# Six of sixteen score tiles a head take another way from PSUM to the exponential: bfloat16 scores, a GpSimd add, one exponential for two tiles

## The chip, the cores and the metric

The program runs on one core of one Trainium2 chip. The metric is device time in microseconds (us), the median of several runs. A profile is one execution taken by the hardware profiler; its times count from the start of that execution's span.

## The reference

A transformer block on 2048 rows of 640 numbers: a layer norm with a conditioned scale and shift, attention with 32 heads of width 128 against a cache of 2048 keys and values, a gated residual, and then a second part with a mixer and an MLP, which the change doesn't touch. What matters here is the attention:

```python
q = (x @ wq).reshape(B, Sq, H, Dh).transpose(0, 2, 1, 3)
scores = jnp.einsum('bhqd,bhkd->bhqk', q, k_cache) * Dh ** (-0.5)
p = _softmax(scores, axis=-1)
o = jnp.einsum('bhqk,bhkd->bhqd', p, v_cache)
return o.transpose(0, 2, 1, 3).reshape(B, Sq, H * Dh) @ wo
```

Inputs and weights are bfloat16. The softmax is taken as exp(score - maximum); its sum comes out of the product with the values, to which a column of ones is appended, and the division follows at the end.

## The kernel before, in words

The kernel is written for the five engines' own queues. A helper class `Prog` keeps a list of operations for each engine in the order in which the program text adds them, and derives every wait from the keys that an operation reads (`r=`) and writes (`w=`). An engine runs its list strictly in order, so an operation that waits holds back all that stands behind it on that engine.

**Loop.** The attention is one loop over steps `s` (L552). There are 32 heads with 16 tiles each, 512 tiles in all; a tile is 128 queries against all 2048 keys. Step `s` starts tile `s` and finishes tile `s - PVD` with `PVD = 8`. I call tiles by their place in the head, 0 to 15. In step `s` each engine gets:

- **TensorE**: for each of two halves of the keys, the scores of tile `s` (two 128x512 matmuls, L301 and L15, into a half of the PSUM tile `Sps`), the product of the probabilities of tile `s - 8` with half of the values (eight matmuls, L314), and a piece of other work where one is due: a fifth of the next head's query projection (L246) or four 128x128 transposes (L262). The scores' half may only be overwritten when VectorE has read it.
- **VectorE**: for each half, one instruction (L594) that reads 1024 columns of scores from PSUM, multiplies by -SCALE, writes them as float32 into `negS`, and accumulates the minimum of them. `negS` has three slots, used in turn, one a tile. So the write of tile `s` waits until the exponential of tile `s - 3` has read its slot.
- **GpSimd**: the smaller of the two halves' minima (L604), 128x1. Further down in the step, the normalisation of a finished tile: L462 for each tile, before the first of four L455 (a reciprocal), after the last of four L469, a store to DRAM.
- **ScalarE**: at every second step the copy of two finished output tiles out of PSUM (L585, into `Of`), then evacuations of queries (L253) and transposed probabilities (L271) where they are due, then the exponential of tile `s` (L607): it reads `negS` with scale -1 and the minimum as bias (a 128x1 operand), and writes bfloat16 probabilities into slot `s % 10` of the ring `Pb`.
- **SyncE** issues the DMA transposes of the probabilities (L231) from `Pb` to the ring `PTs`, for two tiles at once where the two are neighbours, else for one.

**Tiles transposed by TensorE.** In each head tiles 3 and 10 are transposed by TensorE; in every fourth head (`h % 4 == 1`) tile 2 as well. `PE_STEPS` says at which step. Each such tile has two evacuations of 1024 columns: most by ScalarE (L271); VectorE does the second one of tile 2 and of tile 3 (L273, by `by_dve`), 40 in all.

The order of the work is thus written out by hand: nothing is reordered by a scheduler. After the loop come the output projection and the second part of the block.

Of the kernel before, what the change touches and what calls it, by code (L numbers as in the profile page):

```python
# [7 lines left out]
ACT = mybir.ActivationFunctionType  # L8
# [115 lines left out]
def bass_adaLN_cond__mha_block_cached__mixer_s_mlp__prompt_kernel(  # L124
# [7 lines left out]
    NQT = SQ // 128  # L132
# [13 lines left out]
    with ExitStack() as es:  # L146
# [11 lines left out]
        if True:  # L158
            with ExitStack() as es1:
                sb1 = lambda name, shape, dt: es1.enter_context(nc.sbuf_tensor(name, shape, dt))  # L160
                RP = 10
                PVD = 8
                PE_STEPS = ({3: 6, 10: 13}, {2: 5, 3: 7, 10: 14})
                kind = lambda h: 1 if h % 4 == 1 else 0
                US = KT * (SQ + 4)
                sb1("pad", [128, 32], F32)
                ring = sb1("ring", [128, 2 * RP, SK], BF16)
                negS = sb1("negS", [128, 3, SK], F32)
                wo = sb1("wo", [128, H, D], BF16)
                kv = sb1("kv", [128, 2 * SK + 2 * NKT * 130 + 2 * KT * 128 + 2 * SQ], BF16)  # L170
                small = sb1("small", [128, 4 * NQT + 32], F32)
                hTx = sb1("hTx", [128, US], BF16)
                Of = sb1("Of", [128, 4, 2, 130], F32)
# [4 lines left out]
                nm0, nm1, nm, rl = [small[:, 4 * NQT + 8 * i:4 * NQT + 8 * i + 8] for i in range(4)]  # L178
# [8 lines left out]
                Pb = ring[:, 0:RP]  # L187
# [22 lines left out]
                G = Prog(nc, es1, "a")  # L210
# [61 lines left out]
                    else:  # L272
                        G.op("vector", lambda v: v.tensor_copy(dst, src), r=[("J", jb)], w=[("PT", g % RP, r)])  # L273

                by_dve = lambda g, r: r == 1 and g % NQT in (2, 3)
                PIECES = []
                for steps in PE_STEPS:
                    taken = [u for j in steps.values() for u in range(2 * j, 2 * j + 4)]
# [68 lines left out]
                if H > 1:  # L347
# [8 lines left out]
                     r=["id0"], w=["ident"])  # L356
# [3 lines left out]
                for k in range(KT):  # L360
                    G.op("gpsimd", lambda g, k=k: g.tensor_scalar(out=s_bc[:, k, :], in0=ones_f, scalar1=c_f[:, k:k + 1],
                                                                  scalar2=1.0, op0=ALU.mult, op1=ALU.mult),
                         r=["onesf", "cf"] + WRK, w=[("sbc", k)])
# [78 lines left out]
                def mod_rows(i):  # L442
                    n0, n1 = MROW[i]
                    bank = PO[:, (i % 2) * 512:(i % 2) * 512 + n1 - n0]

                    def f(t):
                        for k in range(KT):
                            ins = t.matmul(bank, s_bc[:, k, :], wmodr[:, k, n0:n1], start=(k == 0), stop=(k == KT - 1))
                        return ins
                    G.op("tensor", f, r=[("sbc", k) for k in range(KT)] + [("wm", 1)] + WRK, w=[("O", i % 2)])  # L450
                    G.op("scalar", lambda a: a.copy(mod_bc[:, n0:n1], bank), r=[("O", i % 2)], w=[("mod", i)])
# [35 lines left out]
                w2 = negb[:, 2 * H * 128:2 * H * 128 + KT * D].rearrange("p (k n) -> p k n", k=KT)  # L487
                us = hTx[:, 0:US].rearrange("p (k q) -> p k q", k=KT)
                nT = kv[:, 0:KT * SQ].rearrange("p (t k q) -> p t k q", t=NQT, k=KT)
# [59 lines left out]

                YB = [Sps[:, 0:1024], Sps[:, 1024:2048]]  # L550
                LAG = 4
                for s in range(NG + PVD + LAG):  # L552
                    h, j = divmod(s, NQT)
                    g_ = s - PVD
                    evacs = []
                    if s <= 2:
                        for i in ((0,), (1, 2), range(3, len(MROW)))[s]:
                            mod_rows(i)
                    if s == 3:
                        G.op("gpsimd", lambda g: g.tensor_scalar(  # L560
                            out=mod_bc[:, 2 * D:3 * D], in0=mod_bc[:, 2 * D:3 * D], scalar1=1.0, scalar2=1.0, op0=ALU.add, op1=ALU.mult),
                            r=[("mod", i) for i in range(len(MROW))], w=["mod"])
                    for half in range(2):
                        if s < NG:
                            qk(s, half)
                        if half == 0 and s in (NG + PVD - 5, NG + PVD - 4):
                            b0 = a_pe(0, None if s == NG + PVD - 5 else b0, (s - NG - PVD + 5,))
                        if half == 0 and s == NG + PVD - 2:
                            b1 = a_pe(1, None, (0,))
                        if 0 <= g_ < NG:  # L570
                            pv(g_, half)
                        if s == 0 and half == 1:
                            q_head0(NQC - 1)
                        if h + 1 < H and 2 * j + half in PIECES[kind(h)]:
                            cc, q = PIECES[kind(h)][2 * j + half]
                            q_piece(h + 1, cc, q)
                            if q == KT - 1:
                                evacs.append((q_evac, h + 1, cc))
                        for g, r in t_of(s):
                            t_piece(g, r, half)  # L580
                            if half == 1:
                                evacs.append((t_evac, g, r))
                    if 0 <= g_ < NG and g_ % 2 == 1:
                        p = g_ // 2
                        G.op("scalar", lambda a, p=p: a.copy(  # L585
                            Of[:, p % 4].rearrange("p z d -> p (z d)")[:, 0:259], PO[:, (p % 2) * 512:(p % 2) * 512 + 259]),
                            r=[("O", p % 2)], w=[("Of", p % 4)])
                    for fn, x, y in evacs:
                        if fn is q_evac or not by_dve(x, y):
                            fn(x, y)  # L590
                    for half in range(2):
                        if s < NG:
                            r8 = s % 8
                            G.op("vector", lambda v, half=half, s=s, r8=r8: v.tensor_scalar(  # L594
                                out=negS[:, s % 3, half * 1024:(half + 1) * 1024],
                                in0=Sps[:, half * 1024:(half + 1) * 1024],
                                scalar1=-SCALE, scalar2=None, op0=ALU.mult, op1=ALU.min,
                                accum_out=(nm0 if half == 0 else nm1)[:, r8:r8 + 1]),
                                r=[("S", half)], w=[("negS", s % 3), ("nmh", half, r8)])
                    for fn, x, y in evacs:  # L600
                        if fn is t_evac and by_dve(x, y):
                            fn(x, y)
                    if s < NG:
                        G.op("gpsimd", lambda g, r8=r8: g.tensor_scalar(  # L604
                            out=nm[:, r8:r8 + 1], in0=nm0[:, r8:r8 + 1], scalar1=nm1[:, r8:r8 + 1], scalar2=None, op0=ALU.min),
                            r=[("nmh", 0, r8), ("nmh", 1, r8)], w=[("nm", r8)])
                        G.op("scalar", lambda a, s=s, r8=r8: a.activation(  # L607
                            Pb[:, s % RP, :], negS[:, s % 3, :], ACT.Exp, bias=nm[:, r8:r8 + 1], scale=-1.0),
                            r=[("negS", s % 3), ("nm", r8)], w=[("Pb", s % RP)])
                        if not is_pe(s):  # L610
                            if s % 2 == 1 and not is_pe(s - 1):
                                transpose(s - 1, 2)
                            elif s % 2 == 1 or is_pe(s + 1):
                                transpose(s, 1)
                        if j == 2 and h >= 1 and h + 1 < H:
                            load_k(h + 1)
                        if h + 1 == H and j in (2, PVD + 1):
                            i = 0 if j == 2 else 1
                            load_ot(0, OTC[i], OTC[i + 1], i)
                        if j == 6 and h + 2 < H:  # L620
                            load_wq(h + 2)
                        if j == PVD + 1 and h + 1 < H:
                            load_v(h + 1)
                    if 0 <= s - PVD - LAG:
                        gr, z = divmod(s - PVD - LAG, 4)
                        if z == 0:
                            rcp(gr)
                        norm(gr, z)
                    if s == NG:
                        G.op("gpsimd", lambda g: g.memset(mhalf, -0.5), w=["mhalf"] + NEG)  # L630
                        load_ot(0, OTC[2], OTC[3], 2)
                        load_xt(0, 1)
                        load_ot(1, 0, H // 2, 0)
                        load_ot(1, H // 2, H, 1)
                    if s == NG + 2:
                        load_xt(1, NQC)
# [57 lines left out]
                for n in range(KT):  # L694
                    lst = []
                    p = 0
                    while p < 128:
# [8 lines left out]
                        p = pe_  # L706
# [203 lines left out]
```

## Time and profile before

| what | value |
|---|---|
| device time, median of 3 runs | 1572.19 us (1569.15 to 1576.53) |
| span of the profiled execution | 1568.9 us |
| TensorE busy, share of the span | 1472.3 us, 94% |
| VectorE | 1398.3 us, 89% |
| ScalarE | 1275.9 us, 81% |
| GpSimd | 623.0 us, 40% |
| granted TensorE clock, mean | 0.998 |
| first and last start of the score instruction L594 | 35.4 and 1250.6 us |

The profiled execution has no time of its own beside the span that the profile gives; the span lies 0.3 us below the fastest of the three runs. How to read the views: a group of instructions is one line with the source line, the engine, what it writes and reads, how often, its busy time and the mean duration of one, then the time that the engine stood idle just before them and who ended it. A duration runs to the last write, and the next instruction of the same engine may start some 0.1 to 0.2 us earlier; so where engines are packed, the distance from start to start is what counts, and I call it the pitch. The timeline gives starts. The windows give busy time of each engine in a stretch.

### The profile page before, as it was taken

To read this page: it belongs to the slowest core of one execution; us is meant where nothing else is said; L and a number is where in the kernel's file an instruction comes from. 1 tells how busy PE (TensorE), PEld (TensorE's weight loads), DVE (VectorE), ACT (ScalarE), POOL (GpSimd) and SP (SyncE) were. 2 spreads that over 40 slices of the span, in tenths; PEclk is the share of its full clock that TensorE was granted. 3 is DMA by queue.
4 is the path that set the end of the run, shared out by engine and by line. 5 is a ranking of instruction groups with operands and counts; after the bars stand their busy time and mean duration, and the time that the engine had idled before them with its cause. 6 is when DMAs were issued, how large, how long until landed. Compare 5 with 4: busy or idle time off the path is not lost.

```text
span 1568.9 us, 33553 instructions
## 1 busy us (share of the span) xinstructions
PE 1472.3 (94%) x13947; PEld 923.4 (59%) x13175; DVE 1398.3 (89%) x2471; ACT 1275.9 (81%) x1121; POOL 623.0 (40%) x1396
## 2 busy tenths in 40 slices
PE   5899999999999999999999999999999899999999
PEld 3466666666665566566656666566566655554545
DVE  6999999999999999999999999999999937667435
ACT  4999999999999999999999999999999900034230
POOL 0144444444444444444444444444444433323100
PEclk9999999999999999999999999999999999999999
DMA  9999999999999999999999999999999999725100
GB/s 298 239 221 239 237 242 237 233 241 243 237 240 233 239 232 232 240 236 235 229 237 236 233 243 249 226 242 243 235 241 237 238 246 190 157 53 144 38 22 34
DMA packets 1172828, 334.59 MB, mean 213 GB/s; under 512 B 1153280, under 2 KB 1166656, under 8 KB 1172672
## 3 DMA queue, kind: packets, MB, share of 16 engines
q1 hardware_dynamic: 1164192, 311.30, 100.8%
q0 software_dynamic: 6144, 16.79, 3.5%
q10 hardware_dynamic: 2336, 4.34, 0.8%
q8 instruction: 108, 1.77, 0.5%
q14 instruction: 48, 0.39, 0.1%
HBM read 43.48 MB, written 19.40 MB: 40 GB/s over the span
## 4 chain that ended last, share of the span: by engine, by line
ACT 40%; DVE 23%; PE 19%; DMA 9%; issue 7%; POOL 1%; POOLq 0%; DVEq 0%
ACT ring L607 32%; DVE negS L594 20%; DMA ring<-ring 8%; PE Sps L540 8%; PE Sps L847 4%; ACT ring L271 3%; ACT kv L253 2%; ACT Of L585 2%; PE QPp L798 2%; PE Oaug L798 2%; DVE ring L273 1%; PE Sps L783 1%; DVE ring L379 1%; DMA negS<-o_scratch 1%; PE PTp L314 1%
## 5 line engine op out<-in xcount | busy, mean ns | idle before, releaser
L594 DVE TENSOR_SCALAR_CACHE_REDUCE negS<-Sps 128x1024 f32<-128x1024 f32 x1024 | 1177.7, 1224 | 19.4 <-PE Sps L15 18.5
L607 ACT ACTIVATE ring<-negS,small 128x2048 bf16<-128x2048 f32 x512 | 1045.7, 2066 | 13.7 <-POOL small L604 12.5
L314 PEld LDWEIGHTS PTp<-kv,ring 128*128 128x128 bf16 x8192 | 554.1, 98 | 325.0 <-issue 69.6
L314 PE MATMUL PTp<-kv,ring 128*128 128x129 bf16 x8192 | 645.3, 220 | 25.0 <-DMA ring<-ring 23.9
L15 PE MATMUL Sps<-kv 128*128 128x512 bf16 x1024 | 387.9, 379 | 16.8 <-DVE negS L594 9.9
L604 POOL TENSOR_SCALAR small<-small 128x1 f32<-128x1 f32 x512 | 146.4, 286 | 621.8 <-DVE negS L594 621.7
L301 PE MATMUL Sps<-kv 128*128 128x512 bf16 x919 | 354.3, 386 | 27.8 <-DVE negS L594 16.5
L462 POOL TENSOR_SCALAR On<-Of,small 128x128 bf16<-128x128 f32 x512 | 191.0, 373 | 13.0
L301 PEld LDWEIGHTS Sps<-kv 128*128 128x128 bf16 x1024 | 98.1, 96 | 141.7 <-DVE negS L594 121.6
L455 POOL TENSOR_TENSOR small<-Of,small 128x4 f32<-128x4 f32 x128 | 133.1, 1040 | 8.8 <-ACT Of L585 8.7
L469 POOL DMA_DIRECT2D o_scratch<-On x128 | 103.1, 806 | 40.8 <-POOL On L462 37.2
L585 ACT COPY Of<-PTp 128x259 f32<-128x259 f32 x256 | 108.6, 424 | 13.2 <-PE PTp L314 13.2
L246 PE MATMUL Oaug<-hTx,kv 128*128 128x512 bf16 x268 | 101.9, 385 | 3.7 <-DVE hTx L411 3.7
L246 PE MATMUL QPp<-hTx,kv 128*128 128x512 bf16 x259 | 97.7, 382 | 2.6 <-ACT hTx L406 2.1
L728 ACT ACT_TABLE_LOAD x1 | 1.3, 1283 | 112.6 <-POOL hTx L746 112.6
L594 DVE DVE_READ_ACCUMULATOR negS<-Sps 128x1 f32 x1024 | 90.3, 88 | 0.0
L271 ACT COPY ring<-Oaug 128x1024 bf16<-128x1024 bf16 x72 | 77.0, 1069 | 0.0
L641 POOL TENSOR_SCALAR negS<-negS 128x1 f32<-128x1 f32 x48 | 24.2, 504 | 125.2 <-DVE negS L650 125.2
L540 PE MATMUL Sps<-wo,negS 128*128 128x128 bf16 (+1 forms) x503 | 69.9, 298 | 1.2 <-DMA negS<-o_scratch 0.8
L540 PE MATMUL Sps<-wo,hTx 128*128 128x512 bf16 (+1 forms) x502 | 69.3, 297 | 0.5
L851 DVE TENSOR_TENSOR ring<-Sps,ring 128x640 f32<-128x640 f32 x15 | 12.4, 824 | 59.5 <-PE Sps L847 59.5
L655 DVE TENSOR_TENSOR ring<-Sps,mod_bc 128x640 f32<-128x640 f32 x16 | 13.1, 821 | 53.6 <-PE Sps L540 32.9
(88 smaller groups left out, 1052.7 us busy)
## 6 DMA issues: line engine op xcount, KB each, us to landing
kv<-in_A_v_cache_dram SPq DMA_DIRECT2D x32, 512.0 KB, 5.0
o_scratch<-On POOLq DMA_DIRECT2D x128, 128.0 KB, 4.7
kv<-in_A_wq_dram SPq DMA_DIRECT2D x32, 160.0 KB, 3.2
wo<-in_A_wo_dram SPq DMA_DIRECT2D x1, 5120.0 KB, 16.5
ring<-ring SPq DMA_TRANSPOSE x248, 7.1
ring<-in_A_x_dram SPq DMA_DIRECT2D x5, 640.0 KB, 6.6
ring<-in_w_mod_dram SPq DMA_DIRECT2D x1, 3200.0 KB, 13.8
out_dram<-wo SPq DMA_DIRECT2D x15, 160.0 KB, 1.8
```

The lines of the kernel that those rows point to most:

```text
L15: return t.add_instruction(mybir.InstMatmult(name=t.bass.get_next_instruction_name(), ins=[t.lower_ap(rhs), t.lower_ap(lhsT)], outs=[t.low ...
L246: G.op("tensor", lambda t: t.matmul(JB[jb], wq[:, hb, q, :], hT[:, q, cc * 512:(cc + 1) * 512], start=(q == 0), stop=(q == KT - 1)), r=[(" ...
L271: G.op("scalar", lambda a: a.copy(dst, src), r=[("J", jb)], w=[("PT", g % RP, r)])
L301: ins = (t.matmul if c2 == 0 else partial(same_weights, t))(Sps[:, col:col + 512], QT[:, hb, j * 128:(j + 1) * 128], KTs[:, hb, col:col + ...
L314: ins = t.matmul(ob[:, 0:129], PTs[:, b, kt, :], Vaug[:, hb, kt, 0:129], start=(kt == 0), stop=(kt == NKT - 1))
L455: G.op("gpsimd", lambda g: g.tensor_tensor(out=rl[:, 4 * b:4 * b + 4], in0=Of[:].rearrange("p a z d -> p (a z) d")[:, 4 * b:4 * b + 4, 128 ...
L462: G.op("gpsimd", lambda g: g.tensor_scalar(out=On[:, b, z, :], in0=Of[:, 2 * b + z // 2, z % 2, 0:128], scalar1=rl[:, 4 * b + z:4 * b + z ...
L540: ins = t.matmul(YB[b][:, c0:c0 + cw], OTj[pr % 2][:, 2 * hh + z, :], wo[:, hh, c0:c0 + cw], start=(hh == 0), stop=(hh == H - 1))
L585: G.op("scalar", lambda a, p=p: a.copy(Of[:, p % 4].rearrange("p z d -> p (z d)")[:, 0:259], PO[:, (p % 2) * 512:(p % 2) * 512 + 259]), r= ...
L594: G.op("vector", lambda v, half=half, s=s, r8=r8: v.tensor_scalar(out=negS[:, s % 3, half * 1024:(half + 1) * 1024], in0=Sps[:, half * 102 ...
L604: G.op("gpsimd", lambda g, r8=r8: g.tensor_scalar(out=nm[:, r8:r8 + 1], in0=nm0[:, r8:r8 + 1], scalar1=nm1[:, r8:r8 + 1], scalar2=None, op ...
L607: G.op("scalar", lambda a, s=s, r8=r8: a.activation(Pb[:, s % RP, :], negS[:, s % 3, :], ACT.Exp, bias=nm[:, r8:r8 + 1], scale=-1.0), r=[( ...
```

## The change

The tiles 0, 1, 6, 7, 12 and 13 of every head (`merged`) go another way. VectorE writes their negated, scaled scores as bfloat16 straight into the slot of `Pb`, not into `negS`. GpSimd takes the smaller minimum, negates it, and then adds it to all 2048 columns of the tile in place, with a clamp at zero. At the odd tile of the pair, one exponential without a bias operand does both tiles, 4096 columns, in place. The other ten tiles keep their way; they count through the three slots of `negS` by themselves (`nu`). `PVD` becomes 9. VectorE now evacuates the second half of tile 3 only in heads with `h % 4 == 3`; in the other 24 heads ScalarE does it. Lines after the first insertion move down by up to 15; the score instruction is L598 in the changed kernel, the minimum L608, the new add L612, the pair's exponential L618, the single one L621.

```diff
-                PVD = 8
+                PVD = 9
...
+                MERGED = (0, 6, 12)
+                merged = lambda s: s % NQT // 2 * 2 in MERGED
...
-                by_dve = lambda g, r: r == 1 and g % NQT in (2, 3)
+                by_dve = lambda g, r: r == 1 and (g % NQT == 2 or g % NQT == 3 and g // NQT % 4 == 3)
...
                         if s < NG:
                             r8 = s % 8
-                            G.op("vector", lambda v, half=half, s=s, r8=r8: v.tensor_scalar(
-                                out=negS[:, s % 3, half * 1024:(half + 1) * 1024],
+                            dst, key = (Pb[:, s % RP], ("Pb", s % RP)) if merged(s) else (negS[:, nu % 3], ("negS", nu % 3))
+                            G.op("vector", lambda v, half=half, dst=dst, r8=r8: v.tensor_scalar(
+                                out=dst[:, half * 1024:(half + 1) * 1024],
                                 in0=Sps[:, half * 1024:(half + 1) * 1024],
                                 scalar1=-SCALE, scalar2=None, op0=ALU.mult, op1=ALU.min,
                                 accum_out=(nm0 if half == 0 else nm1)[:, r8:r8 + 1]),
-                                r=[("S", half)], w=[("negS", s % 3), ("nmh", half, r8)])
+                                r=[("S", half)], w=[key, ("nmh", half, r8)])
...
-                        G.op("gpsimd", lambda g, r8=r8: g.tensor_scalar(
-                            out=nm[:, r8:r8 + 1], in0=nm0[:, r8:r8 + 1], scalar1=nm1[:, r8:r8 + 1], scalar2=None, op0=ALU.min),
+                        G.op("gpsimd", lambda g, r8=r8, sc=-1.0 if merged(s) else 1.0: g.tensor_scalar(
+                            out=nm[:, r8:r8 + 1], in0=nm0[:, r8:r8 + 1], scalar1=nm1[:, r8:r8 + 1], scalar2=sc, op0=ALU.min, op1=ALU.mult),
                             r=[("nmh", 0, r8), ("nmh", 1, r8)], w=[("nm", r8)])
-                        G.op("scalar", lambda a, s=s, r8=r8: a.activation(
-                            Pb[:, s % RP, :], negS[:, s % 3, :], ACT.Exp, bias=nm[:, r8:r8 + 1], scale=-1.0),
-                            r=[("negS", s % 3), ("nm", r8)], w=[("Pb", s % RP)])
+                        if merged(s):
+                            G.op("gpsimd", lambda g, s=s, r8=r8: g.tensor_scalar(
+                                out=Pb[:, s % RP, :], in0=Pb[:, s % RP, :], scalar1=nm[:, r8:r8 + 1], scalar2=0.0,
+                                op0=ALU.add, op1=ALU.max),
+                                r=[("nm", r8)], w=[("Pb", s % RP)])
+                            if s % 2 == 1:
+                                pair = ring[:, (s - 1) % RP:s % RP + 1].rearrange("p r s -> p (r s)")
+                                G.op("scalar", lambda a, pair=pair: a.activation(pair, pair, ACT.Exp, scale=-1.0),
+                                     w=[("Pb", (s - 1) % RP), ("Pb", s % RP)])
+                        else:
+                            G.op("scalar", lambda a, s=s, r8=r8, n=nu % 3: a.activation(
+                                Pb[:, s % RP, :], negS[:, n, :], ACT.Exp, bias=nm[:, r8:r8 + 1], scale=-1.0),
+                                r=[("negS", nu % 3), ("nm", r8)], w=[("Pb", s % RP)])
+                            nu += 1
```

More of the change, by code (lines that the diff above doesn't have):

```diff
@@ L551, in bass_adaLN_cond__mha_block_cached__mixer_s_mlp__prompt_kernel @@
                 LAG = 4
+                nu = 0
                 for s in range(NG + PVD + LAG):
```

## The prediction

> **What bounds the kernel now.** I read the engines' windows first. The attention loop runs from 35 to 1252 us, and its middle is even, so here is one stretch of 1000 us:
>
> ```profile
> core 0: us, PE busy (x) PEld busy (x) DVE busy (x) ACT busy (x) POOL busy (x), PEclk, DMA share, GB/s
> 200.00:1200.00 1000.00, 945.64 (x9728) 615.45 (x9065) 986.86 (x1719) 989.84 (x823) 460.43 (x1054) 1.00 1.21 237
> ```
>
> VectorE and ScalarE are both busy 99% of it, and the groups of this stretch count 422 exponentials (L607): 2.370 us a tile, 37.92 us a head. Then the waits of the same stretch:
>
> ```profile
> PE PTp L314 <- DMA ring<-ring: 23.5, 35, 1.7
> DVE negS L594 <- PE Sps L15: 12.5, 22, 1.4
> ...
> ACT ring L607 <- POOL small L604: 8.2, 22, 0.8
> ```
>
> Neither engine waits long for anything, and VectorE never for a slot of `negS`. Next the pitches, from the timelines of ScalarE and VectorE:
>
> ```profile
> 607.97 0.49 ACT L585 COPY Of<-PTp 128x259 f32<-128x259 f32 x1
> 608.23 4.02 ACT L607 ACTIVATE ring<-negS,small 128x2048 bf16<-128x2048 f32 x2
> 612.02 0.49 ACT L585 COPY Of<-PTp 128x259 f32<-128x259 f32 x1
> 612.28 2.14 ACT L607 ACTIVATE ring<-negS,small 128x2048 bf16<-128x2048 f32 x1
> 614.18 0.71 ACT L253 CAST kv<-Oaug 128x512 bf16<-128x512 f32 x1
> 614.65 2.14 ACT L607 ACTIVATE ring<-negS,small 128x2048 bf16<-128x2048 f32 x1
> ...
> 623.25 1.16 ACT L271 COPY ring<-Oaug 128x1024 bf16<-128x1024 bf16 x1
> 624.14 2.17 ACT L607 ACTIVATE ring<-negS,small 128x2048 bf16<-128x2048 f32 x1
> ```
>
> ```profile
> 623.42 1.23 DVE L594 TENSOR_SCALAR_CACHE_REDUCE negS<-Sps 128x1024 f32<-128x1024 f32 x1
> ...
> 624.57 0.69 DVE L273 COPY ring<-QPp 128x1024 bf16<-128x1024 bf16 x1
> 625.17 1.22 DVE L594 TENSOR_SCALAR_CACHE_REDUCE negS<-Sps 128x1024 f32<-128x1024 f32 x1
> ```
>
> From start to start: exponential 1.90, output copy 0.26, query cast 0.47, evacuation 0.90; on VectorE 1.144 a half, so 2.29 a tile, and 0.60 for its evacuation. Per head VectorE needs 16 x 2.289 + 1.25 x 0.60 = 37.4, ScalarE 16 x 1.90 + 8 x 0.26 + 4 x 0.47 + 3.25 x 0.90 = 37.3. Both fit 37.92 with half a microsecond to spare.
>
> **What the change takes and gives in work.** 24 evacuations go from VectorE (0.45 us a head less) to ScalarE (0.68 more). Three pairs of exponentials become one of 4096 columns each. By ScalarE's copies (0.47 for 512 columns, 0.90 for 1024: 0.84 ns a column, 0.04 at the start) that is 3.48 against 3.80, 0.96 a head less; 3.80 is the upper end. VectorE's bfloat16 write I take as unchanged: it still reads 1024 float32 columns of PSUM, as in L594. The low end is the 0.60 of L273, which reads 2-byte columns; far off. If nothing waited, a head would take 36.9 on VectorE, 37.0 on ScalarE, and the time would fall by 0.45 x 32 = 14 us.
>
> **The new operation, GpSimd's add of 2048 columns,** is in no row. The nearest are these, and then GpSimd's timeline:
>
> ```profile
> L462 POOL TENSOR_SCALAR On<-Of,small 128x128 bf16<-128x128 f32 x512 | 191.0, 373 | 13.0
> L604 POOL TENSOR_SCALAR small<-small 128x1 f32<-128x1 f32 x512 | 146.4, 286 | 621.8 <-DVE negS L594 621.7
> ...
> L560 POOL TENSOR_SCALAR mod_bc<-mod_bc 128x640 f32<-128x640 f32 x1 | 0.7, 726 | 0.0
> ```
>
> ```profile
> 599.85 1.04 POOL L455 TENSOR_TENSOR small<-Of,small 128x4 f32<-128x4 f32 x1
> 600.99 0.37 POOL L462 TENSOR_SCALAR On<-Of,small 128x128 bf16<-128x128 f32 x1
> ...
> 606.44 0.28 POOL L604 TENSOR_SCALAR small<-small 128x1 f32<-128x1 f32 x1 [1.67 <-DVE negS L594]
> 606.69 0.37 POOL L462 TENSOR_SCALAR On<-Of,small 128x128 bf16<-128x128 f32 x1
> 607.36 0.81 POOL L469 DMA_DIRECT2D o_scratch<-On  x1 [0.29 <-POOL On L462]
> ```
>
> One column takes 0.286, 640 take 0.726: 0.69 ns a column, which 128 columns in 0.373 bear out. So 2048 take 0.286 + 2047 x 0.00069 = **1.70 us**, my value. Bounds: half of that rate's cost a column (2-byte data both ways) 0.99, twice 3.11. In load GpSimd can bear it: 6 x 1.70 on top of 17.5 a head (46% of 37.92).
>
> The GPSIMD Engine Reference of the Trainium skill (§3.1) gives 1.03 cycles an element at 1.2 GHz as the best for simple bodies, so by an estimate from that page an add would take 0.286 + 1.76 = 2.04 and the sum below would come to 1729; L560 here is quicker than that rate allows.
>
> **The wait it adds.** What counts is the latency. Tile 5's write needs the `negS` slot of tile 2 and tile 11's that of tile 8, and in ScalarE's queue the pair's exponential stands ahead of those of 2 and 8. Let T be when VectorE has issued both halves of a pair's second tile. It could start three tiles later at T + 3 x 2.29 = 6.87. GpSimd starts 0.18 after a tile's pitch ends (in the trace L604 at 601.86, where VectorE's next began at 601.68), leaves 0.10 before an instruction that needs its own result, ScalarE follows in 0.02. A slot comes free 2.06 (mean of L607) + 0.10 after its exponential starts.
>
> Pair (6,7). GpSimd: minimum of 6 from -2.11 to -1.83, add -1.73 to -0.03, L462 to 0.34, minimum of 7 to 0.62, add 0.72 to 2.42. ScalarE: pair 2.44 to 5.92, output copy to 6.18, exponential of 8 from there; slot free at 8.34. VectorE idles 8.34 - 6.87 = **1.47**.
>
> Pair (0,1). In step 0 GpSimd also has the store: L462 ends at 0.34, L469 runs 0.63 to 1.44, minimum of 1 to 1.72, add to 3.52. Pair 3.54 to 7.02, output copy and query cast to 7.75, slot free at 9.91: **3.04**.
>
> Pair (12,13) is as late, but only two tiles use `negS` before the next pair: the slot of 14 is free at T + 10.3 and wanted at 11.4. It costs nothing.
>
> Before, the same path took 0.18 + 0.28 + 0.02 + 2.16 = 2.64 of the 4.58 that it had. VectorE's idling isn't made up: every step of the chain starts from VectorE's own last tile, so each head pays it. Behind the waiting VectorE instruction stand the next tiles' scores, and TensorE's score matmuls wait for them; ScalarE, through with its work, idles at the pairs (about 1.0, 2.5 and 0.5 a head).
>
> The 8 heads with `h % 4 == 1` pay more: VectorE's copy of tile 2 lies ahead of tile 7 (0.60), an evacuation of 0.90 gets in front of the exponential of 8, of which 0.15 returns as GpSimd catches up, and ScalarE comes 0.40 late to the next pair: 1.75, or 0.44 on the mean head. VectorE's copies of tile 3 that remain lie within the stall and cost nothing.
>
> **The rest.** `PVD` 9 puts one step of products more behind the last scores: two half-steps of 0.47, 0.9 in all. It gives the transposes 2.3 us more, and the pair (0,1), out at T + 7, lands by T + 14.2 (median 7.2 to landing), while tile 9's step starts after T + 17. So TensorE's 23.5 us of waits for transposes should be gone, and the end doesn't follow them.
>
> **Sum.** Head: 36.62 + 3.04 + 1.47 + 0.44 = 41.57, against 37.92: 3.65. Times 31 heads: 113. Head 0 has no normalisation on GpSimd, so the add ends at 2.26 in both pairs; stalls 1.52 and 1.05, plus 1.3. With 0.9 at the end: **+115 us**. From the profiled span 1568.9 that is 1684; the median of the runs lies 3.3 above the span, so I predict **1687**.
>
> Unknown terms: an add 0.1 longer or shorter counts four times a head, 12 us. If the store doesn't hold GpSimd up, (0,1) gains 0.81: 1662. If the pair's exponential takes 3.80: 2 x 0.32 x 31 more, 1707. If VectorE's merged halves took 0.60 each, each critical pair would reach T 1.09 earlier against a GpSimd that started with its first tile, and (12,13) would save 2.18: 4.4 a head, 1552.
>
> **Rivals.**
> 1. *The add fits.* Without backlog the slots are free at T + 6.48 + x and 6.95 + x for an add of x, so with x up to about 0.45 us the stalls stay under 0.6 a head; then the saved VectorE evacuations show: 1572 - 14 = **1558**, faster. For it: both engines are at 99%, and the exponential does lose 0.96 a head. Against it: 640 columns already take 0.726. With the 1552 of a fast bfloat16 write: 0.07; and 0.03 that it ends within 0.5% (the least that a measurement of this kernel can tell from no change).
> 2. *A quicker add, 0.99.* No backlog on (6,7); stalls 1.62 and 0.60, 2.29 a head less than mine: **1616**. For it: an L354 of 128x128 bfloat16 takes 0.285, less than 0.373 from float32. Against: one instance of another operation. 0.08.
> 3. *A dearer add, 3.11.* GpSimd's own time in a pair then sets everything: 4 x 1.41 x 31 more, **1862**. For it: 2-byte input and a second operation are in no row of this size; GpSimd's memset of 640 2-byte columns takes 0.632, hardly less than 0.726 for float32 read and written. Against: the even 0.69. 0.12, most of it well below 3.11.
> 4. *VectorE isn't held,* because the bfloat16 tiles, which use no slot of `negS`, give ScalarE time to catch up. They do: of a head's ten single tiles only 3, 5 and 11 come to a slot that may be in use. But 5 and 11 are the fourth write in a row with three slots, right behind a pair. It is in the 0.03.
>
> **Chances.** Mine, 1640 to 1740 (adds of 1.35 to 2.1, the store and the exponential either way): 0.70. Faster by over 0.5%: 0.07, within: 0.03, slower: 0.90. The range 1620 to 1755 takes in mine, the upper part of 2 and the lower part of 3, and leaves out 0.2.
>
> **What would show it.** The changed profile should have VectorE idle before L598 released by ScalarE (L621), some 125 us in all; ScalarE idle before L618 released by GpSimd's L612, some 110 us; L612 x192 at about 1.70; L618 x96 at about 3.6 in duration; TensorE's waits for transposes near nothing; and 41 to 43 us a head. If L612 is under 0.5 us, or VectorE shows no wait for ScalarE, the reasoning falls. If the wait is there and the sizes differ, the add or the store was mis-sized.

## The result, and the profile after

The changed kernel takes 2790.96 us (median of 4 runs, 2790.18 to 2791.75) against 1573.14 for the kernel before on the same chip: 1.776 times as long, 95% interval 1.772 to 1.779. That is 1218 us more, where I had forecast 115.

These are the groups of the changed kernel's page that answer to those shown of before (busy time, mean ns of one, then the idle time ahead and what ended it):

```profile
L612 POOL TENSOR_SCALAR ring<-ring,small 128x2048 bf16<-128x2048 bf16 x192 | 1379.1, 7183 | 17.9
...
L598 DVE TENSOR_SCALAR_CACHE_REDUCE negS<-Sps 128x1024 f32<-128x1024 f32 x640 | 746.2, 1221 | 760.2 <-ACT ring L621 717.4
L618 ACT ACTIVATE ring<-ring 128x4096 bf16<-128x4096 bf16 x96 | 347.2, 3616 | 1225.6 <-POOL ring L612 1225.6
L598 DVE TENSOR_SCALAR_CACHE_REDUCE ring<-Sps 128x1024 bf16<-128x1024 f32 x384 | 454.3, 1221 | 460.7 <-PE Sps L15 460.1
```

The first line holds the miss. GpSimd's add takes 7.18 us, not 1.70; its spread (7166 to 7199 ns over all 192) is too small for anything that other engines do to it. The others are as forecast: the pair's exponential 3.6, VectorE's half 1221 ns whether it writes bfloat16 or float32. The windows show the loop's middle, with GpSimd the busiest engine at 80% and the granted TensorE clock down to 0.77:

```profile
600.00:1200.00 600.00, 332.74 (x2952) 204.02 (x2699) 294.45 (x507) 293.56 (x226) 481.99 (x364) 0.77 0.58 117
```

And the waits of the whole execution (total, times, longest):

```profile
ACT ring L618 <- POOL ring L612: 1225.6, 96, 15.1
...
PE PTp L316 <- ACT Of L588: 894.1, 87, 14.2
DVE negS L598 <- ACT ring L621: 717.4, 62, 13.3
DVE ring L598 <- PE Sps L15: 460.1, 95, 15.2
```

All 96 pairs are waited for, 12.8 us each. VectorE's wait for ScalarE, 62 times, is the one that I had worked out: tiles 5 and 11. But there is a third, of nearly the same size, through TensorE: VectorE waits for scores (L15). One of these waits, in VectorE's, ScalarE's and TensorE's timelines:

```profile
1011.83 1.22 DVE L598 TENSOR_SCALAR_CACHE_REDUCE ring<-Sps 128x1024 bf16<-128x1024 f32 x1
...
1025.92 1.23 DVE L598 TENSOR_SCALAR_CACHE_REDUCE ring<-Sps 128x1024 bf16<-128x1024 f32 x1 [12.86 <-PE Sps L15]
```

```profile
1019.55 3.62 ACT L618 ACTIVATE ring<-ring 128x4096 bf16<-128x4096 bf16 x1 [13.93 <-POOL ring L612]
1023.07 0.36 ACT L588 COPY Of<-PTp 128x259 f32<-128x259 f32 x1
```

```profile
1010.17 0.63 PE L316 MATMUL PTp<-kv,ring 128*128 128x129 bf16 x8
...
1011.07 0.38 PE L15 MATMUL Sps<-kv 128*128 128x512 bf16 x1
1023.58 1.03 PE L316 MATMUL PTp<-kv,ring 128*128 128x129 bf16 x8 [12.13 <-ACT Of L588]
...
1024.82 0.63 PE L303 MATMUL Sps<-kv 128*128 128x512 bf16 x1
1025.25 0.63 PE L15 MATMUL Sps<-kv 128*128 128x512 bf16 x1
```

The pair (12,13) waits on ScalarE until its adds are done. Behind it in ScalarE's queue stands the copy of finished outputs, which empties a PSUM bank (a part of the memory that TensorE writes to). TensorE's products at tile 1 of the next head need that bank, and the scores of tile 1's second half stand behind them. VectorE idles 12.9 us, although no slot of `negS` is short. In the heads that follow one with `h % 4 == 1` the stall comes at tile 0 already and is 15.3 us long; there TensorE waits for the bank of a query piece (`PE Oaug L248 <- ACT ring L273`, 14.8 us at most). Counted from start to start, the three stalls of the head shown, at tiles 1, 5 and 11, are 12.95, 10.48 and 12.76 us. My sum with an add of 7.18 would have had none at tile 1, 14.0 at tile 5 and 12.43 at tile 11. A head takes 75 to 79 us.

### The profile page after: what moved, and what is told of

It reads as the page before. It is cut to its first block, busy times and chain, and to the rows that moved or that the text cites. A ratio compares the mean times of both kernels' runs of the same rounds, so it can differ in the third digit from the quotient of the medians.

```text
span 2789.5 us, 33450 instructions
## 1 busy us (share of the span) xinstructions
PE 1682.2 (60%) x14199; PEld 1011.8 (36%) x13175; DVE 1401.8 (50%) x2447; ACT 1275.3 (46%) x1049; POOL 2007.4 (72%) x1588
## 4 chain that ended last, share of the span: by engine, by line
POOL 48%; PE 18%; DVE 16%; ACT 15%; issue 2%; DMA 0%; POOLq 0%; DVEq 0%; SPq 0%
POOL ring L612 43%; ACT ring L618 10%; DVE ring L598 8%; DVE negS L598 7%; PE Sps L542 5%; ACT ring L621 3%; PE PTp L316 3%; POOL small L608 2%; PE Sps L862 2%; PE Sps L303 2%; PE Sps L15 2%; POOL On L464 1%; PE QPp L813 1%; PE Oaug L813 1%; POOL o_scratch L471 1%
## 5 line engine op out<-in xcount | busy, mean ns | idle before, releaser
L612 POOL TENSOR_SCALAR ring<-ring,small 128x2048 bf16<-128x2048 bf16 x192 | 1379.1, 7183 | 17.9
L316 PE MATMUL PTp<-kv,ring 128*128 128x129 bf16 x8192 | 738.8, 240 | 894.1 <-ACT Of L588 894.1
L316 PEld LDWEIGHTS PTp<-kv,ring 128*128 128x128 bf16 x8192 | 637.1, 109 | 1354.6 <-issue 1155.9
L598 DVE TENSOR_SCALAR_CACHE_REDUCE negS<-Sps 128x1024 f32<-128x1024 f32 x640 | 746.2, 1221 | 760.2 <-ACT ring L621 717.4
L618 ACT ACTIVATE ring<-ring 128x4096 bf16<-128x4096 bf16 x96 | 347.2, 3616 | 1225.6 <-POOL ring L612 1225.6
L598 DVE TENSOR_SCALAR_CACHE_REDUCE ring<-Sps 128x1024 bf16<-128x1024 f32 x384 | 454.3, 1221 | 460.7 <-PE Sps L15 460.1
L621 ACT ACTIVATE ring<-negS,small 128x2048 bf16<-128x2048 f32 x320 | 627.9, 2008 | 0.0
L303 PE MATMUL Sps<-kv 128*128 128x512 bf16 x1024 | 439.7, 429 | 58.3 <-DVE negS L598 55.6
L15 PE MATMUL Sps<-kv 128*128 128x512 bf16 x1024 | 429.4, 419 | 0.0
L608 POOL TENSOR_SCALAR small<-small 128x1 f32<-128x1 f32 x512 | 152.9, 299 | 384.1 <-DVE negS L598 228.3
L248 PE MATMUL Oaug<-hTx,kv 128*128 128x512 bf16 x320 | 138.4, 437 | 125.7 <-ACT ring L273 121.9
L457 POOL TENSOR_TENSOR small<-Of,small 128x4 f32<-128x4 f32 x128 | 133.6, 1044 | 57.2 <-ACT Of L588 57.2
L248 PE MATMUL QPp<-hTx,kv 128*128 128x512 bf16 x320 | 132.8, 419 | 1.4 <-ACT hTx L408 0.7
L471 POOL DMA_DIRECT2D o_scratch<-On x128 | 103.8, 811 | 40.8 <-POOL On L464 37.2
L248 PEld LDWEIGHTS Oaug<-hTx,kv 128*128 128x128 bf16 x320 | 34.8, 109 | 132.4 <-issue 121.4
L273 ACT COPY ring<-Oaug 128x1024 bf16<-128x1024 bf16 x72 | 74.5, 1035 | 2.5 <-PE Oaug L264 2.5
L264 PE MATMUL Oaug<-ident,ring 128*128 128x128 bf16 x576 | 66.9, 249 | 10.2 <-ACT ring L621 10.2
## 6 DMA issues: line engine op xcount, KB each, us to landing
ring<-in_w_mod_dram SPq DMA_DIRECT2D x1, 3200.0 KB, 12.8
```

Of the source, the lines that this page charges most:

```text
L15: return t.add_instruction(mybir.InstMatmult(name=t.bass.get_next_instruction_name(), ins=[t.lower_ap(rhs), t.lower_ap(lhsT)], outs=[t.low ...
L248: G.op("tensor", lambda t: t.matmul(JB[jb], wq[:, hb, q, :], hT[:, q, cc * 512:(cc + 1) * 512], start=(q == 0), stop=(q == KT - 1)), r=[(" ...
L303: ins = (t.matmul if c2 == 0 else partial(same_weights, t))(Sps[:, col:col + 512], QT[:, hb, j * 128:(j + 1) * 128], KTs[:, hb, col:col + ...
L316: ins = t.matmul(ob[:, 0:129], PTs[:, b, kt, :], Vaug[:, hb, kt, 0:129], start=(kt == 0), stop=(kt == NKT - 1))
L457: G.op("gpsimd", lambda g: g.tensor_tensor(out=rl[:, 4 * b:4 * b + 4], in0=Of[:].rearrange("p a z d -> p (a z) d")[:, 4 * b:4 * b + 4, 128 ...
L598: G.op("vector", lambda v, half=half, dst=dst, r8=r8: v.tensor_scalar(out=dst[:, half * 1024:(half + 1) * 1024], in0=Sps[:, half * 1024:(h ...
```

## The experiments

**The add by itself.** Ahead of the attention loop of the kernel before, on scratch, one after the other:

```diff
+G.op("gpsimd", lambda g: g.tensor_scalar(out=Pb[:, 0, :], in0=Pb[:, 0, :], scalar1=sc1, scalar2=0.0, op0=ALU.add, op1=ALU.max), r=PK, w=PK)
+G.op("gpsimd", lambda g: g.tensor_scalar(out=Pb[:, 0, :], in0=Pb[:, 0, :], scalar1=sc1, scalar2=1.0, op0=ALU.add, op1=ALU.mult), r=PK, w=PK)
...
```

> The kernel before with fifteen GpSimd instructions put ahead of the attention loop (scratch in negS and in one slot of the ring), while VectorE isn't using either and nothing else runs on GpSimd: the add with clamp of the change (add a 128x1 operand, then max with 0, 2048 bfloat16 columns in place) and variants that differ in one thing each. Their durations are what is read, not the time. Theory A, the second operation is dear: add-then-max takes about 7.2 us in float32 too, add-then-multiply and multiply-then-multiply about 1.7. Theory B, 2-byte input is dear: every bfloat16-input variant takes about 7.2, the float32 ones 1.7. Theory C, the load by other engines stretches it: all take 1.7 to 2.0 here, the change's own form too. The form not in place differs from the one in place only if the overwriting costs. 512 columns take a quarter of 2048 within the fixed 0.3 if the cost is by the column.

GpSimd's groups, in that run:

```profile
L445 POOL TENSOR_SCALAR ring<-ring,small 128x2048 bf16<-128x2048 bf16 x1 | 7.2, 7188 | 0.1
...
L452 POOL TENSOR_SCALAR negS<-negS,small 128x2048 f32<-128x2048 f32 x1 | 7.2, 7152 | 0.1
...
L447 POOL TENSOR_SCALAR ring<-ring,small 128x2048 bf16<-128x2048 bf16 x1 | 5.4, 5446 | 0.1
...
L450 POOL TENSOR_SCALAR ring<-ring,small 128x512 bf16<-128x512 bf16 x1 | 2.0, 1992 | 0.1
L454 POOL TENSOR_SCALAR negS<-negS,small 128x2048 f32<-128x2048 f32 x1 | 2.0, 1972 | 0.1
L446 POOL TENSOR_SCALAR ring<-ring,small 128x2048 bf16<-128x2048 bf16 x1 | 2.0, 1971 | 0.1
...
L451 POOL TENSOR_SCALAR ring<-ring,small 128x512 bf16<-128x512 bf16 x1 | 0.7, 691 | 0.1
```

L445 is the change's own form and L452 the same in float32: both 7.2, so neither the type nor the load matters; not in place it takes 7.16 us. L446 (add, then multiply by 1.0) and L454 (multiply, multiply, float32) take 1.97. B and C fall; A's numbers come out. But L447, the addition alone, takes 5.4, and that fits none of the three: it has no second operation that could be dear. By the column (512 against 2048) the clamped form costs 3.38 ns, the quick one 0.83.

**Which operations are dear.** The same with other pairs of operations.

```diff
+G.op("gpsimd", lambda g: g.tensor_scalar(out=Pb[:, 0, :], in0=Pb[:, 0, :], scalar1=sc1, scalar2=0.0, op0=ALU.add, op1=ALU.add), r=PK, w=PK)
+G.op("gpsimd", lambda g: g.tensor_scalar(out=Pb[:, 0, :], in0=Pb[:, 0, :], scalar1=sc1, scalar2=0.0, op0=ALU.mult, op1=ALU.add), r=PK, w=PK)
...
```

> Again the kernel before with GpSimd instructions ahead of the attention loop, all 2048 bfloat16 columns in place; the two operations and the kind of the first operand are varied. In the first probe add-then-max took 7.19, add alone 5.45, add-then-multiply and multiply-then-multiply 1.97. Theory 1, only a maximum (a comparison) is dear: add-add, multiply-add and add-subtract take about 2.0, everything with max or min 7. Theory 2, only pairs that end in a multiplication are quick, whatever the first operation: subtract-, max- and min-then-multiply 2.0, all others 5 to 7, the single multiplication too. Theory 3, the 128x1 operand is what costs: add of an immediate, then max, 2.0.

```profile
L445 POOL TENSOR_SCALAR ring<-ring,small 128x2048 bf16<-128x2048 bf16 x1 | 7.2, 7195 | 0.1
...
L448 POOL TENSOR_SCALAR ring<-ring,small 128x2048 bf16<-128x2048 bf16 x1 | 7.2, 7157 | 0.1
...
L454 POOL TENSOR_SCALAR ring<-ring,small 128x2048 bf16<-128x2048 bf16 x1 | 5.5, 5458 | 0.1
...
L446 POOL TENSOR_SCALAR ring<-ring,small 128x2048 bf16<-128x2048 bf16 x1 | 2.0, 1972 | 0.1
L457 POOL TENSOR_SCALAR ring<-ring 128x2048 bf16<-128x2048 bf16 x1 | 1.9, 1902 | 0.1
```

All three theories fall. Add-add (L445), max-multiply (L448), and likewise subtract-multiply, min-multiply, multiply-max, max-max, add-min and add-subtract take 7.15 to 7.20; a single operation 5.43 to 5.46, the multiplication (L454) too. Quick are, of all pairs tried, only multiply-multiply, add-multiply and multiply-add (L446). An immediate (a constant in the instruction) in place of the 128x1 operand saves 0.07 (L457), and add-then-max stays at 7.09 with it. Why these pairs are quick and the others not, no run shows.

**The changed kernel with the quick pair.**

```diff
-scalar1=nm[:, r8:r8 + 1], scalar2=0.0, op0=ALU.add, op1=ALU.max)
+scalar1=nm[:, r8:r8 + 1], scalar2=1.0, op0=ALU.add, op1=ALU.mult)
```

> The changed kernel with one edit: the add's second operation is a multiplication by 1.0 in place of the maximum with 0. Theory A (the maximum is dear): the add falls to 1.7 and the time to 1687, the sum that I had made for that duration, if the chain by way of negS is right as well; with 2.04 it would be 1729. Theory B or C (data type or load): the add stays at 7.2 and the time at 2790. A time near 1570 with an add of 1.7 would say that the chain was wrong and only the add's price counted.

1777.45 us, ratio 1.130 (1.127 to 1.132), the add 1972 ns. So 1014 of the 1218 us go with the clamp. With 1.97 in place of 1.70 my sum gives 1687 + 4 x 0.27 x 31 = 1720; 57 are left. VectorE's waits in that run:

```profile
DVE negS L598 <- ACT ring L621: 116.9, 64, 3.5
...
DVE ring L598 <- PE Sps L15: 95.1, 70, 4.7
```

The second is mostly the third stall, in small. The first is less than the chain had: (3.58 + 2.01) x 31 is 173.

**Without the add.**

```diff
-G.op("gpsimd", lambda g, s=s, r8=r8: g.tensor_scalar(out=Pb[:, s % RP, :], ..., op0=ALU.add, op1=ALU.max), ...)
```

> The changed kernel without GpSimd's add: in the six merged tiles of a head the maximum isn't subtracted. All else stays, the bfloat16 write, the pair's exponential, PVD 9. If the add is all that costs (whatever makes it dear), the chain gives slots free just before they are wanted (T + 6.85 against 6.87) and the time falls to 1558, 1545 to 1575. If something else in the change costs too, as a rival has it (the longer exponential late for the output copies, the evacuations that ScalarE took over), it stays above 1590.

1573.07 us, ratio 0.999 (0.998 to 1.001). No cost remains, but no gain either: rival 1's 1558 didn't come. TensorE's waits for transposes in the stretch from 200 to 1200 us are 26.4, against 23.5 before.

**The two small parts alone.**

```diff
-PVD = 8
+PVD = 9
-by_dve = lambda g, r: r == 1 and g % NQT in (2, 3)
+by_dve = lambda g, r: r == 1 and (g % NQT == 2 or g % NQT == 3 and g // NQT % 4 == 3)
```

> The kernel before with only the two small parts of the change: PVD 9, and ScalarE evacuating tile 3's second half in 24 heads. By the pitches ScalarE then needs 37.98 us a head and is the bound: 1573 to 1585. If the later use of the transposes (PVD 9) is worth what TensorE waited for them, it could come out at 1565; a rival in which these parts cost much would show 1600 or more.

1575.46, ratio 1.002 (1.001 to 1.004); ScalarE is busy 1000.00 of 1000 us of the middle stretch. As expected.

**One pair at a time**, with the quick add, to test the chain.

```diff
-MERGED = (0, 6, 12)
+MERGED = (0,)        # or (6,)
```

> The quick add, but only the pair (0,1) is merged in each head. By the chain with an add of 1.97 VectorE idles 3.6 a head at tile 5 (my 3.04 and two adds 0.27 longer): 36.9 + 3.6 against 37.9, plus 80 us, 1650. If the cost is simply shared among the three pairs, a third of 204: 1641. The two differ in the next run.

> The quick add, only the pair (6,7) merged. By the chain VectorE idles 2.0 a head at tile 11 and no store stands in GpSimd's way: 36.9 + 2.0 + 0.4 for the heads with h % 4 == 1 against 37.9, 1610 to 1620, clearly below the run with (0,1) only. If the cost is shared evenly: 1641, the same as that run. What the two leave of the 204 us belongs to the pair (12,13), which I had put at nothing.

1691.12 (1.075, 1.072 to 1.078) and 1643.66 (1.045, 1.042 to 1.047). The second lies where even sharing would have it (1641), but they differ by 47, so the cost isn't shared evenly. The stalls have their forecast sizes. In four heads of the run with (6,7) VectorE idled 2.03, 2.52, 1.80 and 1.44 before tile 11, where the sum says 1.47 + 2 x 0.27 = 2.01; with (0,1), 3.68 in 28 of 32 heads before tile 5, where it says 3.58. Two of those at tile 5, in VectorE's timeline of the run with (0,1):

```profile
803.82 1.23 DVE L598 TENSOR_SCALAR_CACHE_REDUCE negS<-Sps 128x1024 f32<-128x1024 f32 x1 [3.60 <-ACT ring L621]
...
845.00 1.23 DVE L598 TENSOR_SCALAR_CACHE_REDUCE negS<-Sps 128x1024 f32<-128x1024 f32 x1 [3.59 <-ACT ring L621]
```

The bracket holds the idle time; counted from start to start it is 0.08 more.

But both times are 24 to 41 us over what I expected. I had added the stalls to VectorE's own work, 36.9 a head; the heads take 41.7 and 40.1 on the mean. A part of what is missing in the run with (0,1) is VectorE's waits for scores: 19.8 us between 60 and 1240 us, 0.7 a head.

The two runs cost 118 and 71 us over the kernel before, all three pairs 204. That doesn't make 15 us the share of (12,13): the pairs aren't independent, as the next run shows.

**The rest of the 57 us.** With the quick add the heads after those with `h % 4 == 1` take 47.1 on the mean, where the sum has 42.2; these 8 heads make 39 of the 57 us. The others take 42.8 to 44.2, within 0.2 to 0.6 of the sum (44.0 with `h % 4 == 1`). In the long heads TensorE stands at a query piece whose PSUM bank ScalarE empties behind the pair (12,13).

```diff
-by_dve = lambda g, r: r == 1 and (...)
+by_dve = lambda g, r: (r == 1 and (...) or r == 0 and g % NQT == 10 and kind(g // NQT) == 1)
```

> The changed kernel with the quick add (second operation a multiplication), and in the 8 heads with h % 4 == 1 VectorE in place of ScalarE evacuates the first half of tile 10's transposes, after step 14's scores. With the quick add alone the heads after these take 47.1 us against 42.8 for the like of them, and TensorE stands there at the next head's first query piece, whose PSUM bank ScalarE empties behind the pair (12,13). If that queueing is the cause, these heads fall to 43 and the time from 1777 by 8 x 4 to about 1745. Rival: those heads are long because ScalarE has more to do in all; then the evacuation moved (0.9) saves 8 x 1, and 1770 comes out.

1753.83, ratio 1.114 (1.111 to 1.117), nearer to the 1745 of the queueing than to the rival's 1770. These heads fall to 43.0, which is 33 us, while those with `h % 4 == 1` take 0.9 more: net 24. In this run, VectorE's waits of an ordinary head at tiles 1 and 5, and of one of the 8 heads at tile 5:

```profile
214.72 1.23 DVE L599 TENSOR_SCALAR_CACHE_REDUCE ring<-Sps 128x1024 bf16<-128x1024 f32 x1 [1.40 <-PE Sps L15]
...
224.93 1.23 DVE L599 TENSOR_SCALAR_CACHE_REDUCE negS<-Sps 128x1024 f32<-128x1024 f32 x1 [1.79 <-ACT ring L622]
...
312.52 1.23 DVE L599 TENSOR_SCALAR_CACHE_REDUCE negS<-Sps 128x1024 f32<-128x1024 f32 x1 [3.57 <-ACT ring L622]
```

Where nothing stalls at tile 1, tile 5 pays the chain's 3.6; where 1.4 is paid at tile 1, tile 5 pays 1.8. So in an ordinary head the third stall takes the place of about half of the first, and the sum comes out nearly right for a head whose stalls it has in the wrong places.

**Why nothing is gained when the add is gone.** Three kernels: `PVD` 9 alone; and, against the changed kernel, two without GpSimd's add and with one maximum for both tiles of a pair, where the first keeps before's evacuations and the second the change's:

```diff
-PVD = 8
+PVD = 9
...
-scalar1=nm1[:, r8:r8 + 1], scalar2=sc, op0=ALU.min, op1=ALU.mult),
+scalar1=nm1[:, r8:r8 + 1], scalar2=nm[:, r8 - 1:r8] if second else None, op0=ALU.min, **(dict(op1=ALU.min) if second else {})),
...
-G.op("scalar", lambda a, pair=pair: a.activation(pair, pair, ACT.Exp, scale=-1.0),
+G.op("scalar", lambda a, pair=pair, r8=r8: a.activation(pair, pair, ACT.Exp, bias=nm[:, r8:r8 + 1], scale=-1.0),
```

> The kernel before with PVD 9 alone. With PVD 9 and the moved evacuations TensorE no longer waited for transposes and ScalarE was busy 100% of the middle stretch, at 1575.5. Here ScalarE needs 37.3 and VectorE 37.4 a head of the 37.9 that it takes. If the half microsecond that is missing comes from transposes that land late, 1557 to 1565. If it comes from VectorE and ScalarE getting in each other's way over the three slots, 1570 to 1575.

> The changed kernel without GpSimd's add, but with the softmax kept safe in another way: the pair's exponential takes as bias the maximum over both tiles' keys for each partition, which GpSimd forms with one more 128x1 minimum. VectorE keeps all 40 evacuations as before the change; PVD 9. ScalarE then needs 37.3 - 0.96 + 0.3 = 36.6, VectorE 37.4. If VectorE's work bounds it, 1557 to 1565. In the run without the add TensorE still waited for transposes and nothing was gained; if that rival bound holds here too, 1568 to 1575.

> The same with the change's own split of the evacuations: ScalarE 37.3, VectorE 36.9 a head. Bound by ScalarE's work: 1557 to 1565, as the run before; bound by late transposes, as the run without the add was: 1570 to 1575.

1573.68 (ratio 1.001, 1.000 to 1.002), 1578.79 (1.003, 1.002 to 1.005) and 1576.46 (1.002, 1.001 to 1.003). The 1557 to 1565 came in none of the three; the first lies in the other range that I had given, the second and third above both. Less work for ScalarE brings nothing here, nor does a later use: with PVD 9 alone TensorE waits 30.3 us for transposes in the stretch from 200 to 1200 us, before 23.5.

> The run with PVD 9 alone, and from the second head on the DMA transpose of tiles 14 and 15 is left out (their products are then formed from older transposed tiles): one of six pairs of transposes a head less, nothing else moved. Everything that took work from VectorE or ScalarE stood at 37.9 us a head, where their own work is 37.0 to 37.4. If the transposes are what holds it there, the head falls to VectorE's 37.4 and the time to about 1557. If it is the order of the work on TensorE, VectorE and ScalarE, it stays at 1570 to 1576.

```diff
-if s % 2 == 1 and not is_pe(s - 1):
+if h >= 1 and j in (14, 15):
+    pass
+elif s % 2 == 1 and not is_pe(s - 1):
```

1556.17, ratio 0.989 (0.987 to 0.991). The middle stretch of it, and of the run with PVD 9 alone, engines in the order PE, PEld, DVE, ACT, POOL:

```profile
200.00:1200.00 1000.00, 979.93 (x10068) 636.95 (x9210) 1000.00 (x1747) 999.95 (x837) 468.42 (x1070) 1.00 1.07 213
```

```profile
200.00:1200.00 1000.00, 941.21 (x9702) 611.65 (x9039) 984.12 (x1715) 987.28 (x822) 457.66 (x1050) 1.00 1.21 236
```

With a sixth of the pairs left to older data, VectorE and ScalarE are never idle, and the time is the 1557 that I had put on their own work. So with PVD 9 alone the DMA transposes hold the loop at its 38.0 us a head. They don't hold every head alike: from the second on, with them the heads run from 37.2 to 39.3, without the sixth they are even, 37.2 or 37.8 (the heads with `h % 4 == 1`). Whether the transposes hold by their number or by when they land, the run doesn't tell apart. That they hold the run without the add too is likely from its waits, but not tested there. The last three runs give TensorE 8 tiles more to transpose, with the whole computation done:

```diff
-kind = lambda h: 1 if h % 4 == 1 else 0
+kind = lambda h: 1 if h % 2 == 1 else 0
```

> The kernel before with one edit: TensorE transposes tile 2 in every second head in place of every fourth, 8 tiles of 440 less for the DMA transposes, at the price of 8 x (0.90 on ScalarE and 0.60 on VectorE): both then need 37.5 a head, TensorE up to 36.8 in these heads. If the transposes hold the loop, a sixth of the relief of the run with 62 tiles left out (17 us for 62): 2 to 3 us faster at best, and ScalarE's 37.5 of 37.9 leaves room for it; 1568 to 1573. If the engines' own work counts, 1575 to 1582.

> The version with one maximum for a pair (no GpSimd add, VectorE keeps its evacuations, PVD 9), and TensorE transposes tile 2 in every second head. ScalarE then needs 36.8, VectorE 37.5. If transposes and ScalarE together held that version at 1579, it falls to 1565 to 1573; if the pair's exponential, which lets the first tile's transpose start late, is what holds it, it stays at 1575 to 1580.

> The same with the change's split of the evacuations (ScalarE 37.4, VectorE 37.1). If VectorE's work is what bounds the run before this one, this is the faster of the two by up to 10 us; if ScalarE's, the slower.

On the kernel before: 1568.88, ratio 0.997 (0.996 to 0.999), the only version with all its work that beat it, by 3.5 us. With one maximum for a pair: 1582.18 (1.006, 1.004 to 1.007) and 1585.45 (1.008, 1.006 to 1.009), slower than without the edit and above both of my ranges. I had put 1575 to 1580 on the pair's late first transpose as the cause; it is not shown, and what holds those two versions stays open. Their traces have a candidate that I didn't test: in the stretch from 200 to 1200 us TensorE waits 26 times, once a head, for a query bank that ScalarE empties (19.6 and 19.3 us), against 0.7 us in the kernel before with the same edit. That is the third stall's way again.

## Why the prediction was wrong, point by point

- **The step that failed: "0.286 + 2047 x 0.00069 = 1.70 us, my value", with 3.11 as the upper bound.** It is 7.18. I took the price of a column from rows of the same instruction name and looked for a dependence on width and type. It depends on the two operations: L462 of the kernel before is multiply-multiply and L560 add-multiply, both quick pairs; add-max was in no row. The bound of "twice" stood without a reason of its own; rival 3 named "2-byte input and a second operation" as not in the rows, but not which operation, and L560 has a second one. What the rows could have told: every wide GpSimd tensor_scalar of the kernel before has a multiplication by 1.0 as its second operation, which computes nothing. Taking the clamp out is worth 1014 of 1218 us.
- **"L560 here is quicker than that rate allows"** was wrong as well. The Trainium skill's GPSIMD Engine Reference, §3.1, gives 1.03 cycles an element at 1.2 GHz for simple bodies, 0.86 ns by an estimate from it; the quick pairs here measure 0.83 a column, close to it. The add-then-max of this case, 3.38 ns, is four times that, and the measurement decides. L560 looked quicker because it has no 128x1 operand, while the 0.286 that was taken off it came from an instruction that has one: from L560 to L457, both without, it is 0.84 ns a column.
- **The chain by way of `negS`** was right in mechanism, and in size where one pair stands alone: 2.01 against 1.44 to 2.52, 3.58 against 3.68. With all three pairs the stall at tile 5 is smaller than the sum's, 1.8 to 1.9 in most heads with the quick add and about 10.6 for 14.0 in the changed kernel, as a part of it is paid at tile 1. With 7.18 the sum gives 1687 + 4 x 5.48 x 31 = 2367.
- **"Pair (12,13) ... costs nothing"** failed. It holds for the slots of `negS`; I hadn't followed ScalarE's queue behind the waiting exponential to the PSUM banks that it empties and TensorE needs. At 7.18 that is the third stall, 13 to 15 us a head. The 424 us from 2367 to 2791 are 13.7 a head, but that this is the stall's own size is chance: VectorE's waits for scores come to 503 us (460.1 + 42.8), small waits behind the stalls among them, and its waits for ScalarE to 717, some 100 less than the 819 of the sum.
- **"In load GpSimd can bear it"**: at 7.18 six adds make 43 of its 61 us a head, and it became the busiest engine.
- **Rival 3, the dearer add,** was the right direction with 0.12, but its 1862 ended at a bound that the operation's real price left far behind. **Rival 1** was wrong in more than its chance: a free add gives 1573, not 1558; what holds the loop then is most likely the DMA transposes. "So TensorE's 23.5 us of waits for transposes should be gone" gave `PVD` 9 the credit, wrongly: with it alone they are 30.3, without the add 26.4. In the changed kernel they are gone because other stalls give the transposes time.
- Right were the bfloat16 write (1221 ns both), the pair's exponential (pitch 3.52 against 3.48), the small parts (1575, with ScalarE busy without a break), and the sign.

## What to carry to other kernels

Price an instruction by its operations as well as its shape, and look for what all known quick instances share; a multiplication by one that computes nothing is a hint. Don't add up stalls that were worked out one at a time: a wait early in the chain can take the place of a later one. When an instruction is made to wait, go through everything behind it in its queue, PSUM banks that it frees included, before a wait is called free. And two engines at 99% don't prove that their work is the bound: leave a piece of the third party's work out, and see whether they reach 100%.

## What the runs showed of the hardware that I had not expected

- GpSimd's tensor_scalar on 128x2048 with a 128x1 operand: 1.97 us for multiply-multiply, add-multiply and multiply-add, 5.43 to 5.46 for a single operation, 7.15 to 7.20 for all other pairs tried. The add-max, add-multiply and multiply-multiply forms cost the same in bfloat16 and float32; the others were run in bfloat16 alone. A second operation that does nothing, the multiplication by 1.0, makes an addition 2.8 times as quick.
- After a wait of 12 us TensorE's 512-column matmuls start 0.43 us apart, not 0.22, for some 4 us (1023.6 to 1027.4 in the changed kernel's timeline), and the granted clock over the loop is 0.77. The Trainium skill, TensorE: Matmul & The Clock Gate, Part 1, has the array at half rate after an idle window of about 3.4 us and back at full rate after as long of work; the timeline agrees. Behind the three stalls of the head shown VectorE waits for scores another 0.83, 0.85 and 0 us; that the clock is all of the reason isn't shown.
